# Whole-float32 scores for the first two tiles, and earlier transposes in the first batch of a top-k attention kernel with two feed-forward layers

## The chip, the core and the metric

The kernel runs on one core of a Trainium2 chip. The metric is the device time of one execution in microseconds (us). Engines: PE (TensorE, matrix products and transposes), PEld (its weight loads), DVE (VectorE), ACT (ScalarE), POOL (GpSimd), SP (SyncE, which here only issues transfers).

## What is computed

```python
def _attn_ref(q, k, v):            # (4, 8, 576, 64) each
    scores = scale * np.matmul(q, k.transpose(0, 1, 3, 2))
    kth = np.partition(scores, -32, axis=-1)[..., -32:-31]
    scores = np.where(scores >= kth, scores, -1e9)
    scores = scores - np.max(scores, axis=-1, keepdims=True)
    attn = np.exp(scores)
    attn = attn / (np.sum(attn, axis=-1, keepdims=True) + 1e-09)
    return np.matmul(attn, v)
def _moe_ref(x, w_in, w_out):      # x (2304, 512), w_in (512, 2048), w_out (2048, 512)
    h = np.maximum(x @ w_in, 0.0)
    return h * h @ w_out
def _moe2_ref(x, w_in, w_out):
    h = x @ w_in
    return np.maximum(0.01 * h, h) @ w_out
# reference: _moe2_ref(_moe_ref(rows of _attn_ref)), all float32
```

## The kernel before

Attention. The 8 heads go in 4 pairs of heads. `UNITS` cuts the four batches into runs of rows; a unit with one head pair gives tiles of 128 score rows (576 columns each), 144 in all, and two tiles make one of 72 pairs. A pair has 16 slots. In slots 0 to 13 DVE finds the 32 largest scores of the pair's two tiles, four rounds of MAX8 (`L829`) and three of MATCH_REPLACE8 (`L831`) each. Behind that ACT and POOL drop the other scores and take the exponential (`drop`, `expo_sum`, `L298` to `L303`), PE transposes the result (`pt_main` `L317`, `pt_left` `L330`; ACT copies it out of PSUM), and PE multiplies it with the values.

The scores (`scores`, `L279`) are computed with products of two float32r parts: queries and keys are loaded as float32 (`load_q` `L248`, `load_k` `L204`), and `split_hi` and a subtraction cut each into a high part and the rest, `split_q` and `split_k`. For the first head pair ACT makes the high parts (`L116`) and DVE the rests (`L258`, `L241`). The key tile holds two copies of the 64 rows of a head, one above the other, so that high part and rest lie in the upper and lower 64 partitions, and two products (with `q` high, with `q` rest) give a half tile of scores. ACT copies each half tile out (`L280`). Tiles 0 to 3 are those of the first head pair and the first 256 rows, 0 and 1 of its first head.

Units 0 to 2 (the first batch, `NATIVE` = 3) transpose whole float32 values and multiply them with the values in whole float32 (`av`, `L401`); the result is scaled and becomes the feed-forward's input, `xn` (`L432`) and its parts `xh`, `xl` (`x_out`). The later units scale first (`norm`, `L312`), split what was transposed (`L322`, `L323`) and use split values (`av_split`, `L412`).

Feed-forward. The 2304 rows form six blocks of 512, 256, 384, 512, 256 and 384 rows. A block and layer is 16 steps: products with `w_in` (12 of `L580`), the activation (ACT, POOL or DVE), products with `w_out` one step later (`L618` in layer 0, `L620` in layer 1). The weights arrive as 64-bit floats and are converted on the way in by ACT (`L513`, `L514`, `L523`), DVE (SCALAR_TENSOR_TENSOR, `L518`, `L519`) and POOL (`L526`); block 0 does so, then the results are read back from DRAM. Block 0 is ready with the eighth `xn` (unit 1, last head pair).

What sets the order. Every piece of attention is put in a slot by hand: `at(slot, function, ...)` (`L739` to `L782`). The loop at `L814` goes through the slots, issues what stands in them, and between them as many feed-forward pieces as a rate asks for. When a block becomes ready, feed-forward work that is still open is issued first (`L841`). The framework's scheduler then orders the instructions of each engine by its own estimate, with attention pieces at a higher priority, so the order on an engine is near the order of the slots but not the same. An engine does its instructions strictly in that order.

Of the kernel before, what the change touches and what calls it, by code (L numbers as in the profile page):

```python
# [38 lines left out]


NATIVE = 3

EARLY = (2, 3)
FILL = (2, 245)
# [27 lines left out]
def topk_attention_moe_moe2_kernel(  # L72
# [11 lines left out]
    D = v.shape[-1]  # L84
    P = 128
# [8 lines left out]
    PE, ACT, DVE, POOL, SP = nc.tensor, nc.scalar, nc.vector, nc.gpsimd, nc.sync  # L94
# [31 lines left out]
    uhs = []  # L126
    tiles = []
    for u in units:
        for hp in range(NHP):
            n = u["n"]  # L130
            uh = dict(u=u, hp=hp, n=n, b=u["b"], first=(u["t0"] == 0), ti=len(tiles), idx=len(uhs),
                      c0=P * (hp % 2) if n == 64 else 0)
# [14 lines left out]
    def direct(uh):  # L147
        return uh["b"] not in EARLY
# [4 lines left out]
    def split(uh):  # L153
        return uh["u"]["i"] >= NATIVE

# [35 lines left out]
    def at(slot, fn, *a):  # L191
        events.setdefault(slot, []).append((fn, a))
# [4 lines left out]
    def load_k(b, hp, st):  # L197
        if b in EARLY:
            KT[b, hp] = ahead.tile([P, 2, S], R, tag="KTa", name="KTa", bufs=KPB)
        else:  # L200
            KT[b, hp] = pool.tile([P, 2, S], R, tag="KT", name="KT", bufs=4)
        x = ahead if b in EARLY else pool
        st["k"] = x.tile([P, 2, S], F, tag="kraw", name="kraw", bufs=1 if b in EARLY else KRB)
        SP.dma_start(st["k"], k[b, hp])  # L204

    VT = {}
# [54 lines left out]
    def scores(t, half):  # L261
        uh = t["uh"]
        d = uh["qs"]
        kt = KT[uh["b"], uh["hp"]]
        if half == 0:
            if direct(uh):
                t["s"] = sbufs[t["i"] % NS]
            else:
                t["s"] = ahead.tile([P, S], F, tag="stage", name="stage", bufs=NST)
        ks = slice(half * HALF, (half + 1) * HALF)  # L270
        mm = [(x[:, h, c:c + P], kt[:, h, ks]) for h, c in t["parts"] for x in d]
        if not direct(uh):
            ps = stage_psum.tile([P, 512], F, tag="sp", name="sp", bufs=SPB)
        elif uh["b"] == 0:
            ps = stage_psum.tile([P, 512], F, tag="sd", name="sd", bufs=SDB)
        else:
            ps = bank()
        for i, (l, r) in enumerate(mm):
            PE.matmul(ps[:, 0:HALF], lhsT=l, rhs=r, start=i == 0, stop=i == len(mm) - 1)  # L279
        ACT.activation(t["s"][:, ks], ps[:, 0:HALF], AF.Copy)  # L280
        if half == 1 and not direct(uh):
            t["sd"] = dram.tile([P, S], F, tag=f"sd{t['i']}", name=f"sd{t['i']}")
            SP.dma_start(t["sd"], t["s"])
# [370 lines left out]
    for uh in uhs:  # L654
        b, hp, i = uh["b"], uh["hp"], uh.get("di")
        z = score_slot(uh["ti"])
        if uh["first"] and direct(uh):
            st = {"i": i}
# [8 lines left out]
        if (b, hp) not in vdone or split(uh) and VTB < NHP:  # L667
            assert not uh["u"]["i"] < NATIVE <= units[max(x["i"] for x in units if x["b"] == b)]["i"]
            vdone.add((b, hp))
# [36 lines left out]
    for n, key in enumerate(keys):  # L706
        ks = [(0, load_k, (*key, held[key]))]
# [9 lines left out]
        if n + 1 < len(keys):  # L717
            nk = keys[n + 1]
            ks = [(0, load_k, (*nk, held[nk]))]
# [15 lines left out]
    for p in range(NPAIRS):  # L735
        pr = dict(t=tiles[2 * p:2 * p + 2], p=p)
        pairs.append(pr)
        z = 16 * p
        for i, t in enumerate(pr["t"]):  # L739
            if direct(t["uh"]):  # L740
                at(z - DLEAD + 5 * i, scores, t, 0)
                at(z - DLEAD + 2 + 5 * i, scores, t, 1)
            else:
                at(z - LEAD + i, load_s, t)
            if i == 0:
                at(z + 14, shifts, pr)
            at(z + 14 + i, drop, pr, i)
            at(z + 16 + i, expo_sum, pr, i)
            if split(t["uh"]):
                at(z + 20 + i, norm, pr, i)  # L750
            at(max(z + 20 + 3 * i, z + 21 + i), pt_main, t)
        at(z + 18, recip, pr)
        at(z + 26, pt_left, pr)
    rslot = [None] * len(blocks)

    def rmark(uh, z):
# [6 lines left out]
    for uh in uhs:  # L763
        if split(uh):
            za, z = 16 * (uh["lastA"] // 2) + 30, 16 * (uh["last"] // 2) + 30
            at(za, av_split, uh, 0)
            at(z + 2, av_split, uh, 1)
            z += 4
            at(z, x_out, uh, (0, 1))
            rmark(uh, z)  # L770
            continue
        apart = uh["n"] > P and uh["n"] % P and uh["ti"] % 2 == 0
        for hs in ((0,), (1,)) if apart else ((0, 1),):
            z = 16 * (uh["lastA"] // 2 if hs == (0,) else uh["last"] // 2) + 30
            nq = 2 * len(hs)
            for i in range(nq):
                at(z + i, av, uh, hs, i)
            at(z + nq, x_out, uh, hs)
        z += nq
        if uh["u"]["i"] == NATIVE - 1 and uh["hp"] == NHP - 1:  # L780
            at(z, open_late)
        rmark(uh, z)  # L782
# [30 lines left out]
    last = max(events)  # L813
    while slot <= last:  # L814
        p, i = divmod(slot, 16)
        if slot >= 0 and p < NPAIRS:
            pr = pairs[p]
# [7 lines left out]
            t = pr["t"][x]  # L825
# [79 lines left out]
```

## Time and profile before

| | us |
|---|---|
| runs, median (lowest to highest) | 1217.16 (1215.74 to 1218.06) |
| profiled execution | 1214.43 |
| its span, first to last instruction | 1212.6 |
| PE busy | 1135.6 (94%) |
| DVE busy | 946.5 (78%) |
| ACT busy | 908.9 (75%) |
| POOL busy | 728.1 (60%) |
| mean granted clock of PE | 0.983 of full speed |

The table says that PE is the fullest engine over the whole span. It is a mean over stages: attention alone at first, then attention and feed-forward together, then feed-forward alone. Which engine sets the time is read stage by stage, from the busy time in stretches and from what an engine waited for.

### The profile page before, as it was taken

The page shows a single profiled execution, that of the slowest core. Times are in us where ns is not written, and L with a number is a line of the kernel's source. Part 1 is how long each engine was busy: PE and PEld are TensorE (multiplying, and loading weights), DVE is VectorE, ACT ScalarE, POOL GpSimd, SP SyncE. Part 2 cuts the span into 40 slices and gives each one's busy share as a digit, 9 for nine tenths or more (in the row PEclk, how much of TensorE's full clock was granted, in tenths as well). Part 3 has the DMA queues.
Part 4 walks back from the last instruction along what each step waited for, and adds up shares of the span by engine and source line. Part 5 has one row for each costly group of instructions (what it writes and reads, how often), then busy time and mean ns, then how long its engine had stood idle before and what let it go on. Part 6 is the DMA issues. An engine that isn't in the chain of part 4 may idle for free.

```text
span 1212.6 us, 20357 instructions
## 1 busy us (share of the span) xinstructions
PE 1135.6 (94%) x6388; PEld 992.6 (82%) x6388; DVE 946.5 (78%) x1944; ACT 908.9 (75%) x2019; POOL 728.1 (60%) x868
## 2 busy tenths in 40 slices
PE   4788878999789989999999998999999999999998
PEld 3666765887578879989999996888788899998997
DVE  7999999778888899999999999999999920110122
ACT  6889899989999988887877777777777764334322
POOL 7998977667689985477656684545576642004300
PEclk9999997999989999999999999999999999999999
DMA  9665566878889988889988787667576589879974
GB/s 305 232 224 196 197 197 255 279 273 303 307 281 301 315 281 270 291 283 397 343 297 293 279 274 258 213 221 236 182 233 230 192 270 368 259 247 343 350 253 137
DMA packets 110522, 323.24 MB, mean 267 GB/s; under 512 B 17488, under 2 KB 25680, under 8 KB 110416
## 3 DMA queue, kind: packets, MB, share of 16 engines
q1 hardware_dynamic: 107776, 317.24, 77.1%
q10 hardware_dynamic: 2640, 4.72, 1.1%
q8 instruction: 51, 0.84, 0.3%
q14 instruction: 55, 0.45, 0.1%
HBM read 254.54 MB, written 67.37 MB: 265 GB/s over the span
## 4 chain that ended last, share of the span: by engine, by line
PE 54%; ACT 17%; DVE 12%; DMA 4%; POOL 3%; issue 3%; ACTq 0%; SPq 0%; POOLq 0%; DVEq 0%
PE h L580 22%; PE acc L618 11%; PE acc L620 11%; DVE m L829 5%; DVE w L831 4%; PE att L412 3%; PE att L317 3%; ACT e L303 2%; ACT att L514 2%; ACT e L298 1%; ACT wc L513 1%; PE att L401 1%; ACT s L280 1%; ACT stage L280 1%; DVE PTs L323 1%
## 5 line engine op out<-in xcount | busy, mean ns | idle before, releaser
L580 PE MATMUL h<-xh,wi 128*128 128x512 f32 (+2 forms) x1280 | 349.8, 345 | 10.5 <-ACT gb L598 4.4
L829 DVE MAX8 m<-w 128x8 f32<-128x576 f32 x432 | 313.2, 747 | 1.6
L580 PEld LDWEIGHTS h<-xh,wi 128*128 128x128 f32 x1280 | 227.5, 191 | 39.3 <-ACT gb L598 6.2
L601 POOL TENSOR_TENSOR gl<-ga,gh 128x512 fp32r<-128x512 f32 (+2 forms) x160 | 163.0, 1018 | 118.8 <-ACT gh L600 54.0
L299 POOL TENSOR_TENSOR e<-s,e 128x576 f32<-128x576 f32 x144 | 203.2, 1432 | 26.7 <-ACT e L298 24.2
L831 DVE MATCH_REPLACE8 w<-m,w 128x576 f32<-128x576 f32 x288 | 213.1, 742 | 0.8
L580 PE MATMUL h<-xl,wi 128*128 128x512 f32 (+2 forms) x640 | 206.8, 341 | 2.8 <-DVE xl L632 2.6
L618 PE MATMUL acc<-gh,wo 128*128 128x512 f32 (+2 forms) x768 | 154.8, 341 | 0.4 <-ACT gh L600 0.4
L620 PE MATMUL acc<-wo,gh 128*128 128x512 f32 x576 | 151.1, 397 | 0.7 <-ACT gh L600 0.6
L599 POOL TENSOR_TENSOR ga<-ga,gb 128x512 f32<-128x512 f32 (+2 forms) x80 | 81.3, 1017 | 117.0 <-ACT gb L598 116.6
L618 PEld LDWEIGHTS acc<-gh,wo 128*128 128x128 f32 x768 | 125.0, 189 | 10.6 <-ACT gh L600 1.1
L580 PEld LDWEIGHTS h<-xl,wi 128*128 128x128 f32 x640 | 121.0, 190 | 15.3 <-DVE xl L632 5.1
L600 ACT ACTIVATE gh<-ga 128x512 fp32r<-128x512 f32 (+2 forms) x192 | 100.3, 522 | 35.6 <-POOL ga L599 24.2
L303 ACT ACTIVATE e<-e,kf 128x576 f32<-128x576 f32 x144 | 112.4, 781 | 15.6 <-POOL e L299 14.2
L620 PEld LDWEIGHTS acc<-wo,gh 128*128 128x128 f32 x576 | 104.2, 189 | 19.6 <-ACT gh L600 1.2
L298 ACT ACTIVATE e<-s,kf 128x576 f32<-128x576 f32 x144 | 105.8, 777 | 15.4 <-POOL kf L291 13.5
L829 DVE MAX8 m<-s 128x8 f32<-128x576 f32 x144 | 104.5, 747 | 11.9 <-ACT s L280 10.8
L590 ACT ACTIVATE ga<-h 128x512 f32<-128x512 f32 (+2 forms) x96 | 46.8, 487 | 82.5 <-PE h L580 81.8
L831 DVE MATCH_REPLACE8 w<-m,s 128x576 f32<-128x576 f32 x144 | 106.8, 742 | 0.3
L317 PE MATMUL att<-ident,e 128*128 128x128 f32 x576 | 90.3, 285 | 13.1 <-ACT e L303 9.2
L317 PEld LDWEIGHTS att<-ident,e 128*128 128x128 f32 x576 | 70.6, 145 | 27.4 <-ACT e L303 14.9
L312 ACT ACTIVATE e<-e,rc 128x576 f32<-128x576 f32 x108 | 78.0, 770 | 13.6 <-DVE rc L308 13.5
(93 smaller groups left out, 2150.8 us busy)
## 6 DMA issues: line engine op xcount, KB each, us to landing
wi<-wd SPq DMA_DIRECT2D x160, 512.0 KB, 5.0
wo<-wd SPq DMA_DIRECT2D x160, 512.0 KB, 5.2
wraw<-in_w_dram SPq DMA_DIRECT2D x64, 512.0 KB, 5.7
sd<-stage SPq DMA_DIRECT2D x72, 288.0 KB, 2.8
s<-sd SPq DMA_DIRECT2D x72, 288.0 KB, 5.0
wd<-wi SPq DMA_DIRECT2D x32, 512.0 KB, 5.3
wd<-wo SPq DMA_DIRECT2D x32, 512.0 KB, 5.5
kraw<-in_k_dram SPq DMA_DIRECT2D x16, 576.0 KB, 4.6
```

The lines of the kernel that those rows point to most:

```text
L298: ACT.activation(e, x, AF.Relu, bias=pr["kf"][:, i:i + 1], scale=-FAR)
L299: cur["pool"] = POOL.tensor_tensor(e, x, e, op=OP.subtract)
L303: ACT.activation(e, e, AF.Exp, bias=pr["nb"][:, i:i + 1], scale=0.125, accum_out=pr["sum"][:, i:i + 1])
L317: PE.transpose(ps[:, j * P:(j + 1) * P], t["e"][:, j * P:(j + 1) * P], ident)
L580: PE.matmul(h[:, 0:n], lhsT=wi[:, w, c * P:(c + 1) * P], rhs=x[c][y][:, 0:n], start=cnt == 0, stop=cnt == 3 * NK - 1)
L599: POOL.tensor_tensor(a[:, 0:n], a[:, 0:n], b[:, 0:n], op=OP.subtract)
L600: ACT.activation(gh[:, 0:n], a[:, 0:n], AF.Copy)
L601: (DVE if j >= GLD else POOL).tensor_tensor(gl[:, 0:n], a[:, 0:n], gh.bitcast(F)[:, 0:n], op=OP.subtract)
L618: PE.matmul(acc[c][:, 0:n], lhsT=wo[:, w, cs], rhs=g[:, 0:n], start=first, stop=last)
L620: PE.matmul(acc[c], lhsT=g[:, cs], rhs=wo[:, w, :], start=first, stop=last)
L829: cur["dve"] = DVE.max(out=m8[:, x, 8 * r:8 * r + 8], in_=t["s"] if r == 0 else t["w"])
L831: cur["dve"] = DVE.match_replace(out=t["w"], in_to_replace=m8[:, x, 8 * r:8 * r + 8], in_values=t["s"] if r == 0 else t["w"], imm_value=NEG)
```

## The change

Two edits. First, `load_k` loads the keys of the first head pair in two transfers, one for each head, and keeps the loaded tile; `scores` computes tiles 0 and 1 as one product for each half tile, from the loaded queries and keys in whole float32 (64 partitions), in place of two products of split parts. The split parts are still made, for tiles 2 and 3 and for the later units. Second, in the units of the first batch `pt_main` moves from slots 21 and 23 of a pair to 19 and 21, `pt_left` from 26 to 23, and `av` and `x_out` start four slots earlier (26 instead of 30). In later units `pt_main` of the pair's first tile moves from slot 21 to 20.

```diff
@@ load_k
+        if (b, hp) == (0, 0):
+            uhs[0]["kraw"] = st["k"]
+            for h in range(2):
+                SP.dma_start(st["k"][:, h], k[b, hp, :, h])
+            return
         SP.dma_start(st["k"], k[b, hp])
@@ scores
         mm = [(x[:, h, c:c + P], kt[:, h, ks]) for h, c in t["parts"] for x in d]
+        if t["i"] < WHOLE:                 # WHOLE = 2
+            c = t["i"] * P
+            mm = [(uh["q"][0:D, 0, c:c + P], uh["kraw"][0:D, 0, ks])]
@@ slots of a pair
-            at(max(z + 20 + 3 * i, z + 21 + i), pt_main, t)
+            at(z + (20 if split(t["uh"]) else 19) + (3 if split(t["uh"]) else 2) * i, pt_main, t)
         at(z + 18, recip, pr)
-        at(z + 26, pt_left, pr)
+        at(z + (26 if split(pr["t"][0]["uh"]) else 23), pt_left, pr)
@@ units of the first batch
-            z = 16 * (uh["lastA"] // 2 if hs == (0,) else uh["last"] // 2) + 30
+            z = 16 * (uh["lastA"] // 2 if hs == (0,) else uh["last"] // 2) + 26
```

New lines shift the numbers: `L280` of before is `L291` after, `L829` is `L840`, `L580` is `L591`.

ACT at the very start, before. `q_80` are the first head pair's queries, `q_86` the second's, `KT` the first head pair's split keys, `s_104` and `s_105` the scores of tiles 0 and 1.

```order
L116 ACT_TABLE_LOAD
L116 ACTIVATE q_80<-qraw 128x256 x2
L116 ACTIVATE KT<-kraw 128x576 x2
L116 ACTIVATE q_86<-qraw 128x256 x2
L280 ACTIVATE s_104<-sd 128x288 x2
L280 ACTIVATE s_105<-sd 128x288 x2
```

The same place after:

```order
L118 ACT_TABLE_LOAD
L118 ACTIVATE q_80<-qraw 128x256 x2
L118 ACTIVATE KT<-kraw 128x576
L118 ACTIVATE q_86<-qraw 128x256 x2
L291 ACTIVATE s_104<-sd 128x288
L118 ACTIVATE KT<-kraw 128x576
L291 ACTIVATE s_104<-sd 128x288
L291 ACTIVATE s_105<-sd 128x288 x2
```

The second half of the keys moved behind two query copies and a copy of scores.

DVE before the eighth `xn`, which makes block 0 ready, before. `m` and `w` belong to the top-k, `wc` to the conversion of weights.

```order
L829 MAX m_2842<-w 128x8
L829 MAX m_2556<-w 128x8
L831 MATCH_REPLACE w<-m_2842,w 128x576
L308 RECIPROCAL rc<-sum 128x2
L831 MATCH_REPLACE w<-m_2842,s_105 128x576
L829 MAX m_2842<-w 128x8 x2
L831 MATCH_REPLACE w<-m_2842,w 128x576
L432 TENSOR_TENSOR xn<-att,rb 128x256
L831 MATCH_REPLACE w<-m_2842,w 128x576
L518 SCALAR_TENSOR_TENSOR wc<-att,wc 128x512
```

The same place after:

```order
L842 MATCH_REPLACE w<-m_2892,s_105 128x576
L529 SCALAR_TENSOR_TENSOR wc<-att,wc 128x512 x2
L842 MATCH_REPLACE w<-m_2892,w 128x576
L840 MAX m_2892<-w 128x8
L530 SCALAR_TENSOR_TENSOR wc<-att,wc 128x512 x2
L840 MAX m_2892<-w 128x8
L842 MATCH_REPLACE w<-m_2892,w 128x576
L443 TENSOR_TENSOR xn<-att,rb 128x256
L319 RECIPROCAL rc<-sum 128x2
L842 MATCH_REPLACE w<-m_2892,w 128x576
```

From the program's start to this `xn` there are 261 top-k instructions (MAX and MATCH_REPLACE) in both orders, 8 conversions of weights before and 12 after.

PE around the first transposes of pair 29, before. `e_112` and `e_113` are the pair's two tiles, `h` and `acc` are feed-forward work.

```order
L580 MATMUL h<-xh_2890,wi 128x256 x4
L317 MATMUL att<-ident,e_112 128x128 x4
L618 MATMUL acc<-gh,wo 128x256 x8
L618 MATMUL acc<-gl,wo 128x256 x4
L317 MATMUL att<-ident,e_113 128x128 x4
L279 MATMUL att<-KT,q_80 128x288
```

The same place after:

```order
L423 MATMUL att<-PTs,VT 128x320
L591 MATMUL h<-xh_2867,wi 128x256
L328 MATMUL att<-ident,e_112 128x128 x4
L591 MATMUL h<-xh_2867,wi 128x256
L629 MATMUL acc<-gh,wo 128x256 x7
L290 MATMUL att<-KT,q_80 128x288
```

Counted from the start, 960 feed-forward products (`L580`, `L618`, `L620`) stand before these transposes before and 935 after. At other pairs, counted in the same way (before, after): pair 20: 348, 360; 21: 408, 420; 22: 480, 488; 27: 792, 780; 28: 867, 852; 30: 1020, 1013; 31: 1100, 1088; 36: 1374, 1338; 47: 1962, 1941; 48: 2016, 1995; 49: 2067, 2046; 52: 2163, 2163.

## Rows read from the trace of the kernel before

**Rows 1.** The page, part 1: busy us, share of the span, instructions.

```profile
PE 1135.6 (94%) x6388; PEld 992.6 (82%) x6388; DVE 946.5 (78%) x1944; ACT 908.9 (75%) x2019; POOL 728.1 (60%) x868
```

**Rows 2.** Busy time by stretch: us, each engine, granted clock, DMA share, GB/s.

```profile
210.00:240.00 30.00, 30.00 (x156) 25.21 (x156) 22.19 (x42) 28.55 (x61) 21.77 (x23) 1.00 0.84 281
...
400.00:500.00 100.00, 95.76 (x642) 87.14 (x641) 92.25 (x187) 89.75 (x207) 70.00 (x83) 1.00 0.85 284
...
500.00:600.00 100.00, 98.34 (x667) 92.22 (x666) 98.78 (x210) 80.73 (x189) 66.84 (x88) 1.00 0.93 342
...
1000.00:1100.00 100.00, 100.00 (x653) 99.65 (x652) 12.40 (x24) 40.78 (x91) 9.88 (x14) 1.00 0.85 290
```

**Rows 3.** Timeline, 0 to 10 us: start, us, engine, line, operation, [idle before].

```profile
1.46 0.58 SPq L204 DMA_DIRECT2D kraw<-in_k_dram  x1
...
4.35 0.72 ACT L116 ACTIVATE q<-qraw 128x256 fp32r<-128x256 f32 x2 [2.33 <-DMA qraw<-in_q_dram]
...
6.25 1.25 ACT L116 ACTIVATE KT<-kraw 128x576 fp32r<-128x576 f32 x2 [1.19 <-DMA kraw<-in_k_dram]
...
6.97 1.43 DVE L241 TENSOR_TENSOR KT<-kraw,KT 64x576 fp32r<-64x576 f32 x2 [1.42 <-ACT KT L116]
...
7.42 0.70 ACT L116 ACTIVATE q<-qraw 128x256 fp32r<-128x256 f32 x2
...
7.79 1.24 POOL L118 TENSOR_SCALAR q<-qraw 128x256 fp32r<-128x256 f32 x2 [3.90 <-DMA qraw<-in_q_dram]
...
9.65 0.76 DVE L829 MAX8 m<-s 128x8 f32<-128x576 f32 x1 [1.25 <-ACT s L280]
```

**Rows 4.** Timeline, 202 to 209 us, DVE and PE.

```profile
203.20 0.42 DVE L432 TENSOR_TENSOR xn<-att,rb 128x256 f32<-128x256 f32 x1
...
204.90 1.41 PE L580 MATMUL h<-xh,wi 128*128 128x512 f32 x5 [0.57 <-ACT xh L433]
...
208.17 0.66 PE L317 MATMUL att<-ident,e 128*128 128x128 f32 x4 [0.95 <-DVE wc L519]
```

**Rows 5.** Groups of DVE, 214 to 500 us: xcount | busy us, mean ns | idle.

```profile
L518 DVE SCALAR_TENSOR_TENSOR wc<-att,wc 128x512 uint32<-128x512 uint32 x57 | 38.8, 683 | 25.5 <-ACT att L514 23.8 <-POOL wi L526 1.4
```

**Rows 6.** Line L317, transposes: summary, then their count up to three times.

```profile
L317 PE MATMUL att<-ident,e x576: 269/273/478, 28.1 to 984.8; 128*128 128x128 f32 x192
...
0.00:214.00 214.00, 26.22 (x136) 16.80 (x136) 0.94 0.69 229
...
0.00:440.00 440.00, 37.05 (x208) 26.00 (x208) 0.97 0.78 261
...
0.00:697.00 697.00, 61.02 (x384) 46.55 (x384) 0.98 0.81 278
```

**Rows 7.** Chain that ended last, 690 to 705 us: start, us, what.

```profile
691.07 2.08 PE h L580 x12
...
693.27 2.10 PE acc L620 x9
...
695.84 0.46 ACT PTs L322
...
698.99 2.84 POOL e L299 x2
```

**Rows 8.** Busy time by stretch, at the block change.

```profile
740.00:750.00 10.00, 7.14 (x42) 5.64 (x40) 10.00 (x22) 7.99 (x16) 5.21 (x6) 1.00 0.76 228
...
750.00:760.00 10.00, 7.29 (x29) 5.87 (x30) 9.78 (x22) 5.53 (x11) 1.43 (x3) 0.83 0.66 225
```

**Rows 9.** Busy time by stretch, before the feed-forward starts.

```profile
190.00:195.00 5.00, 3.99 (x13) 2.89 (x13) 5.00 (x11) 5.00 (x10) 3.77 (x3) 0.50 1.02 411
...
195.00:200.00 5.00, 4.94 (x14) 3.21 (x13) 5.00 (x11) 4.06 (x10) 4.96 (x5) 0.61 0.57 224
```

**Rows 10.** Timeline of PE, 189 to 202 us.

```profile
189.95 1.65 PE L580 MATMUL h<-xh,wi 128*128 128x512 f32 x3 [0.95 <-ACT stage L280]
...
195.27 6.30 PE L401 MATMUL att<-PT,VN 128*128 128x256 f32 x18
```

More of the change, by code (lines that the diff above doesn't have):

```diff
@@ L41 @@
 NATIVE = 3
+WHOLE = 2
 EARLY = (2, 3)
```

## The prediction

> **What bounds the kernel now.** I read the summary of engines first, then busy time by stretch, then the chain that ended last, then the timeline at the two places that the change touches. The reader is to see three stages. TensorE (PE) is busy 1135.6 of 1212.6 us [rows 1], so any time saved must come out of its 77 us of idleness or follow an earlier start. Up to about 205 us there is attention alone, and VectorE (DVE), which runs the top-k, sets the pace. From 210 us on the feed-forward work lies between the attention, PE is full (30.00 of 30) and DVE falls to 22.19 of 30; from 500 us both are full (98.34 and 98.78 of 100); at the end only feed-forward work is left and PE is at 100.00 of 100 [rows 2]. The end is a fixed amount of PE work behind the last attention, so a gain must make the attention or the PE queue earlier before that. Which of the two holds between 440 and 700 us is the open question: the chain runs over PE until 695 us and then over POOL [rows 7], though DVE has no slack either.
>
> **The sum's base.** The profiled execution took 1214.43 us (span 1212.6 and 1.8 around it); the median of the three runs, 1217.16, is 2.7 above. I take the terms from the profile and subtract them from the median.
>
> **Part 1, the first two tiles as whole float32.** Removed: eight products of split operands and, for the first tile, their wait for the split keys. Added: four products of whole operands and one more DMA. It is tempting to count the start of PE, 7.8 us, but DVE's queue decides: the first MAX8 (9.65) still stands behind the subtraction of both halves of the keys, which ends at 6.97 + 1.43 = 8.40, so at most the 1.25 us that DVE then waits can go [rows 3]. What is late next is the second half of the keys. Bytes that had landed: 256 KB of queries by 4.35, 832 KB by 6.25 (keys of 576 KB), 1344 KB by 7.79 (two more queries) [rows 3]. In the new order the first half (544 KB) comes by about 5.3, the second head pair's queries (800 KB) by 6.1, the second half (1088 KB) by 7.0: estimates along these three rows. ScalarE (ACT), by the order, then does one key half (to 5.9), two query copies of 0.36 (to 6.85), a score copy of 0.4 (to 7.25), the other half of 0.63 (to 7.9), and DVE's subtraction of 0.72 ends at about 8.65 [rows 3]. So the first MAX8 is at 8.7 instead of 9.65: **-0.9**. Ends: -1.25 if nothing is in the way, -0.4 if the second half lands only at 7.79.
>
> The four new products are not shown by the trace. Nearest are the whole-float32 products with the values: 18 instructions in 6.30 us at a granted clock near 0.6, two for each product, so 0.70 us for 256 columns and 0.79 for 288 [rows 9, 10]. Two of them from 5.3 end at 6.9 and are copied by 8.3, before DVE wants them; at half that price they would be just as hidden. If they cost twice as much they end at 8.5, the copy at 8.9, and a quarter of a microsecond of the gain is lost. The added DMA issue is some 0.6 us on SP's queue [rows 3], and what stands behind it (keys and queries of later head pairs, one load now also waiting for PE to have read the whole queries) comes one or two issues later, up to 1.2 us; the third pair's top-k, over ten microseconds on, hides it. If it didn't, DVE would wait that long once.
>
> **Part 2, transposes and products of the first batch moved by 2 to 4 slots.** In the order the feed-forward's start does not move against the top-k: 261 top-k instructions stand before the eighth `xn`, which completes the first block's input, before and after. So the slots alone are worth nothing there; that `xn` starts at 203.20 with no idle time of DVE before it, so DVE's queue sets it, and the first full step follows at 204.90 [rows 4]. But 12 instead of 8 SCALAR_TENSOR_TENSOR of the weight conversion now stand before it: 4 x 0.683 = 2.7 us [rows 5] in a stretch in which DVE never idles. A part comes back, because PE waits 0.95 us for just such a conversion at 208.17 [rows 4]. **+1.7**; ends 0 (the conversions fall into gaps of DVE) and +2.7.
>
> Then the order of attention against feed-forward on PE. At the first transposes of a pair the changed order has, against before, 12 more feed-forward products done at pairs 20 and 21, but fewer from pair 27 on: 12 to 25 fewer at pairs 27 to 29, 36 at pair 36, and exactly 21 fewer at pairs 47, 48 and 49. Twenty-one is one whole step of the 384-row block, 12 products of 2.08 us and 9 of 2.10 [rows 7]: 4.2 us of PE time that the attention no longer waits for. Pairs 0 to 47 have been transposed by 697 us [rows 6], where the chain leaves PE for POOL [rows 7]. The step isn't saved, it is done later, but there is a place for it: between 740 and 760 us PE idles 5.6 us because the next block isn't ready [rows 8]. So where PE sets the pace up to 697 us, this is **-4.2**. The other end is taken where DVE sets it: DVE is already full from about 440 us, 26 pairs transposed [rows 6]; there the lag is about 14 products (the mean over pairs 27 to 31), of a 256-row block. By the 384-column products (2.08 for 12 [rows 7]) I estimate two thirds of 0.17, 0.12 us each: -1.7. I take -4.2, because the chain, the only view that orders the two, is on PE there.
>
> Sum: -0.9 + 1.7 - 4.2 = **-3.4**, 1217.16 - 3.4 = **1213.8 us**.
>
> **Rivals.**
> *DVE holds from 440 us.* For it: 98.78 busy of 100 from 500 us [rows 2]. Against: the chain. Then -0.9 + 1.7 - 1.7 = -0.9: 1216.3.
>
> *The feed-forward starts earlier after all.* Seventeen pairs are transposed between 28.1 and 214 us [rows 6], 10.9 us for a pair of 16 slots, so four slots are 2.7 us. For it: the products stand earlier, the weights are ready. Against: 261 in both. It would replace the +1.7 by -2.7: -0.9 - 2.7 - 4.2 = -7.8, 1209.4.
>
> *Attention is put behind at pairs 20 to 22 and doesn't recover.* This ends on the slower side. There the order has 12 feed-forward products of 512 columns more before the transposes; nine such took 2.10 us [rows 7], 0.23 each, so PE reaches the attention 12 x 0.23 = 2.8 us later in a stretch where DVE is already down to three quarters [rows 2]. If DVE is what matters from there, its lost time isn't given back: -0.9 + 1.7 + 2.8 = +3.6, 1220.8. It decides if DVE's busy share between 214 and 300 us falls by over 2.4 us and the lag at pair 47 is then used up waiting. Against: PE is the full engine there.
>
> *A low clock at the start of the feed-forward.* From 190 to 195 us the granted clock was 0.50, the 1.2 GHz level, after PE had stood idle before several of its groups, and three feed-forward products took 1.65 us, 0.55 each [rows 9, 10]. If the new order leaves such a gap before the first full step, 12 products cost 12 x (0.55 - 0.23) = 3.8 us more; where DVE holds later on, that is -0.9 + 1.7 + 3.8 - 1.7 = +2.9, 1220.1. The Trainium skill ("TensorE: Matmul & The Clock Gate", section "What's actually happening") says that the throttled clock is the default and activity releases it, so a change that thins out PE's work before a full stretch would pay this; the trace agrees in that the low rows follow idle ones. Against: in the order nothing is taken from PE just before that step.
>
> *The first tile gains nothing,* since the second half of the keys lands later than I estimate: part 1 is 0 and DVE holds: 1217.2.
>
> **How the numbers follow.** This kernel's measurement can't tell less than about 0.2%, 2.4 us, from no change. Forecast 0.40 (0.35 of it beyond 2.4 us, 0.05 within); DVE holds 0.25 (within); earlier start 0.10 (faster); attention behind 0.15 and low clock 0.05 (slower); nothing at the start 0.05 (within). Faster 0.45, same 0.35, slower 0.20. The forecast's own range, with part 1 at either end, the conversions at 0 to 2.7 and the lag at 4.2, is 1211.7 to 1215.3. The range for 8 in 10 goes from 1208.5 (most of the earlier start) to 1220.5 (some of the slower cases): DVE idles 7.8 us in each of the stretches 210 to 240 and 400 to 500 [rows 2], and the many small moves of the order there can give or take a few of them.
>
> **What would show it.** The first MAX8 at 8.4 to 9.2 us, with the second key half's copy as what it follows; at 9.6 part 1 is wrong. The eighth `xn` at about 205.0 (203.2 - 0.9 + 2.7), later than before though its products stand earlier; at 201 the second rival is right. Pair 47 transposed by about 693.5 instead of 697, and PE's idleness at the block change near 740 to 760 us down from 5.6 to about 1.4 us: that is the step that decides. If it stays at 5.6 and the last stretch is shifted by only a microsecond, DVE holds. Rows with a doubled price in the first ten products after 205 us would show the clock.

## The result, and the profile after

The changed kernel takes 1227.37 us (median of 6 runs, 1225.32 to 1229.59), the kernel before beside it 1217.61 (6 runs): a ratio of 1.0073, interval 1.0055 to 1.0092. It is 9.8 us slower, where 3.4 us faster was forecast; the range ended at 1220.5. The profiled execution took 1229.59 us, its span is 1227.8, 15.2 more than before. The profile before is one of that kernel's shorter executions and the profile after the longest of its six, so differences between the two traces carry some 5 us more than the medians do.

In this execution the start came out as forecast. The timeline of the changed kernel, 0 to 10 us (start, us, engine, line, operation, idle before):

```profile
1.44 0.58 SPq L209 DMA_DIRECT2D kraw<-in_k_dram  x1
...
2.67 0.60 SPq L209 DMA_DIRECT2D kraw<-in_k_dram  x1
...
4.69 2.25 PE L290 MATMUL sd<-kraw,qraw 64*128 64x288 f32 x4 [4.69 <-DMA kraw<-in_k_dram]
...
7.00 0.67 ACT L118 ACTIVATE KT<-kraw 128x576 fp32r<-128x576 f32 x1
...
7.70 0.90 DVE L248 TENSOR_TENSOR KT<-kraw,KT 64x576 fp32r<-64x576 f32 x1 [1.66 <-ACT KT L118]
...
8.64 0.76 DVE L840 MAX8 m<-s 128x8 f32<-128x576 f32 x1
```

The first MAX8 stands at 8.64 instead of 9.65 [rows 3], behind the second half of the keys. That difference is not shown to be the edit's. The same row of the kernel before, unchanged, in its second execution, and of the first edit alone:

```profile
9.07 0.76 DVE L829 MAX8 m<-s 128x8 f32<-128x576 f32 x1 [1.25 <-ACT s L280]
...
9.22 0.76 DVE L840 MAX8 m<-s 128x8 f32<-128x576 f32 x1
```

Over the ten traces with the first edit this row stands at 9.27 in the mean (8.64 to 9.97), over the ten without it at 9.26 (8.96 to 9.68).

Then the eighth `xn` and the first full feed-forward step, in the timeline at 209 to 212 us:

```profile
209.54 0.41 DVE L443 TENSOR_TENSOR xn<-att,rb 128x256 f32<-128x256 f32 x1
...
211.30 2.03 PE L591 MATMUL h<-xh,wi 128*128 128x512 f32 x5 [0.63 <-ACT xh L444]
```

Both are 6.4 us later than before (203.20 and 204.90 [rows 4]). Where they went is read from what DVE waited for between 30 and 212 us. (`rc` holds the reciprocals of the sums, `rb` their transposed copy, by which `xn` is scaled; `kf` is the bound below which scores are dropped.) Before (engine, tile, line, what it waited for: us in total, times, longest):

```profile
DVE xn L432 <- ACT rb L366: 1.3, 1, 1.3
DVE rc L308 <- POOL sum L307: 0.6, 1, 0.6
DVE m L829 <- POOL kf L291: 0.5, 1, 0.5
```

After:

```profile
DVE xn L443 <- ACT rb L377: 4.6, 2, 2.8
DVE rc L319 <- POOL sum L318: 1.4, 3, 0.8
DVE m L840 <- POOL kf L302: 1.3, 4, 0.6
```

All rows of the view sum to 3.0 us before and to 7.3 after. So the eighth `xn` is accounted for: 203.2 - 0.4 (DVE has done 0.4 us more by 30 us, which is all that is left by then of the earlier MAX8) + 2.7 (four more conversions ahead of it) + 4.3 (more waiting) = 209.8, measured 209.5. Busy time by stretch says the same. Before (us, PE, PEld, DVE, ACT, POOL, granted clock, DMA share, GB/s):

```profile
0.00:30.00 30.00, 13.83 (x54) 11.36 (x54) 22.50 (x47) 18.13 (x42) 23.82 (x54) 0.97 0.97 304
30.00:212.00 182.00, 152.98 (x827) 120.76 (x827) 178.37 (x381) 164.52 (x436) 155.93 (x198) 0.94 0.65 217
212.00:300.00 88.00, 86.90 (x442) 71.99 (x441) 66.75 (x125) 81.47 (x173) 61.35 (x61) 1.00 0.84 285
300.00:500.00 200.00, 185.99 (x1055) 159.03 (x1054) 177.16 (x345) 184.27 (x398) 151.76 (x159) 0.98 0.86 291
500.00:700.00 200.00, 197.23 (x1249) 186.31 (x1249) 197.92 (x420) 158.25 (x351) 131.69 (x167) 0.99 0.88 312
```

After:

```profile
0.00:30.00 30.00, 16.28 (x52) 12.25 (x53) 22.89 (x47) 17.15 (x39) 23.67 (x54) 0.96 0.89 262
30.00:212.00 182.00, 154.63 (x801) 124.85 (x801) 174.06 (x374) 163.10 (x432) 154.39 (x197) 0.87 0.65 220
212.00:300.00 88.00, 86.63 (x432) 71.67 (x431) 61.31 (x116) 77.43 (x164) 56.92 (x58) 0.98 0.78 278
300.00:500.00 200.00, 183.96 (x989) 153.78 (x988) 173.96 (x336) 182.26 (x388) 152.27 (x157) 0.97 0.83 280
500.00:700.00 200.00, 194.92 (x1256) 182.87 (x1255) 197.50 (x418) 157.42 (x354) 126.35 (x164) 0.99 0.85 303
...
185.00:205.00 20.00, 15.38 (x49) 11.43 (x48) 19.63 (x42) 19.60 (x46) 15.41 (x16) 0.50 0.78 279
...
210.00:240.00 30.00, 29.24 (x144) 23.89 (x145) 22.85 (x45) 26.32 (x57) 19.09 (x21) 0.94 0.72 247
```

Between 30 and 212 us DVE does 4.3 us less, between 212 and 300 us 5.4 less, between 300 and 500 us 3.2 less. With the 0.4 more at the start it is 9.4 us behind by 300 us and 13.0 by 700 us, where the spans of these two traces end 15.2 apart. Its work in all is unchanged (946.5 us before, 945.6 after), so that work comes later, and after 500 us, where DVE and PE have both no slack [rows 2], nothing is given back. Between 212 and 300 us the waits are again of many kinds, for instance in the timeline after:

```profile
256.56 0.17 DVE L319 RECIPROCAL rc<-sum 128x2 f32<-128x2 f32 x1 [3.33 <-POOL sum L318]
258.58 0.23 DVE L443 TENSOR_TENSOR xn<-att,rb 128x64 f32<-128x64 f32 x1 [1.85 <-PE att L412]
...
299.27 0.69 DVE L334 TENSOR_TENSOR PTs<-att,PTs 128x512 fp32r<-128x512 f32 x1 [3.73 <-ACT PTs L333]
```

The largest single wait before 212 us shows how one comes about. After, 142 to 157 us:

```profile
142.19 1.13 ACT L291 ACTIVATE stage<-sp 128x288 f32<-128x288 f32 x3 [1.90 <-DMA sd<-stage]
...
142.66 1.38 PE L290 MATMUL sp<-KTa,q 128*128 128x288 f32 x6 [1.80 <-ACT stage L291]
...
147.92 2.52 PE L412 MATMUL att<-PT,VN 128*128 128x256 f32 x10
...
151.80 2.52 PE L412 MATMUL att<-PT,VN 128*128 128x256 f32 x10
...
154.62 0.38 PE L362 MATMUL att<-ident,rc 128*128 128x128 f32 x2
...
155.30 0.38 ACT L377 ACTIVATE rb<-att 64x256 f32<-64x256 f32 x1
...
155.71 0.42 DVE L443 TENSOR_TENSOR xn<-att,rb 128x256 f32<-128x256 f32 x1 [2.85 <-ACT rb L377]
...
156.05 1.41 DVE L840 MAX8 m<-w 128x8 f32<-128x576 f32 x2
```

Before, the same place:

```profile
148.45 2.52 PE L401 MATMUL att<-PT,VN 128*128 128x256 f32 x10
...
151.27 0.38 PE L351 MATMUL att<-ident,rc 128*128 128x128 f32 x2
...
152.37 0.38 ACT L366 ACTIVATE rb<-att 64x256 f32<-64x256 f32 x1
...
152.78 0.42 DVE L432 TENSOR_TENSOR xn<-att,rb 128x256 f32<-128x256 f32 x1
```

This `xn`, the sixth, stands in DVE's queue behind 198 top-k instructions before and 196 after, nearly the same place, but the second ten products and the transposes of `rc` behind them come 3.4 us later on PE, although their slots are earlier. Part of that is read in the first two rows: ahead of them on PE stand scores of later batches, which wait 1.80 us for ACT, and ACT waits 1.90 us for the staging tile to be written to DRAM; in the trace before there is no such wait for a transfer between 126 and 148 us. DVE reaches `xn`, finds `rb` missing, and the top-k behind it stands still for 2.85 us. The Trainium skill ("PSUM — Partial Sum Buffer", section "Engine vs sequencer instructions") says that the queues of ScalarE, VectorE and GpSimd are strictly first in, first out; this row agrees, for the MAX8 behind `xn` had its input and starts only at 156.05.

The late step, after. Transposes up to 697 us (line `L328`: PE, PEld, clock); then the last eight of pair 47 in PE's timeline, before and after; then the block change, now some 14 us later:

```profile
0.00:697.00 697.00, 63.07 (x375) 47.92 (x376) 0.95 0.79 270
```

```profile
695.20 1.04 PE L317 MATMUL att<-ident,e 128*128 128x128 f32 x8
...
708.93 1.04 PE L328 MATMUL att<-ident,e 128*128 128x128 f32 x8
```

```profile
760.00:770.00 10.00, 7.49 (x37) 5.64 (x36) 9.83 (x21) 8.25 (x18) 4.92 (x6) 0.91 0.79 220
770.00:780.00 10.00, 9.31 (x37) 7.22 (x36) 9.93 (x23) 7.78 (x15) 4.49 (x5) 0.92 0.81 276
```

375 transposes instead of 384 [rows 6], pair 47 done 13.7 us later, and 3.2 us of idle PE at the block change instead of 5.6 [rows 8].

### The profile page after: what moved, and what is told of

The parts are those of the page before. It is cut to its first block, busy times and chain, and to the rows that moved or that the text cites. A ratio compares the mean times of both kernels' runs of the same rounds, so it can differ in the third digit from the quotient of the medians.

```text
span 1227.8 us, 20345 instructions
## 1 busy us (share of the span) xinstructions
PE 1152.6 (94%) x6388; PEld 1005.8 (82%) x6388; DVE 945.6 (77%) x1944; ACT 909.8 (74%) x2019; POOL 727.3 (59%) x868
## 4 chain that ended last, share of the span: by engine, by line
PE 49%; DVE 9%; POOL 1%; ACT 1%; issue 1%; DMA 0%; ACTq 0%; POOLq 0%
PE h L591 22%; PE acc L631 11%; PE acc L629 10%; DVE m L840 4%; PE att L423 3%; DVE w L842 3%; PE att L328 2%; DVE PTs L334 1%; PE att L341 1%; DVE xl L643 0%; PE att L290 0%; DVE PTs L351 0%; POOL gl L612 0%; POOL e L310 0%; DMA out_dram<-y 0%
## 5 line engine op out<-in xcount | busy, mean ns | idle before, releaser
L591 PE MATMUL h<-xh,wi 128*128 128x512 f32 (+2 forms) x1280 | 352.9, 348 | 11.1 <-ACT ga L601 3.0
L840 DVE MAX8 m<-w 128x8 f32<-128x576 f32 x432 | 313.0, 747 | 1.4
L591 PEld LDWEIGHTS h<-xh,wi 128*128 128x128 f32 x1280 | 229.0, 192 | 38.8 <-ACT ga L601 4.1
L591 PE MATMUL h<-xl,wi 128*128 128x512 f32 (+2 forms) x640 | 209.0, 344 | 3.6 <-DVE xl L643 3.4
L591 PEld LDWEIGHTS h<-xl,wi 128*128 128x128 f32 x640 | 122.2, 192 | 17.5 <-DVE xl L643 5.9
L840 DVE MAX8 m<-s 128x8 f32<-128x576 f32 x144 | 104.8, 747 | 6.8 <-ACT s L291 4.5
L328 PE MATMUL att<-ident,e 128*128 128x128 f32 x576 | 94.3, 289 | 11.5 <-ACT e L314 6.5
L328 PEld LDWEIGHTS att<-ident,e 128*128 128x128 f32 x576 | 73.4, 148 | 23.7 <-ACT e L314 10.7
L290 PE MATMUL sp<-KTa,q 128*128 128x288 f32 x320 | 72.6, 355 | 20.0 <-ACT stage L291 14.8
```

Source lines behind the costliest of these rows:

```text
L328: PE.transpose(ps[:, j * P:(j + 1) * P], t["e"][:, j * P:(j + 1) * P], ident)
L591: PE.matmul(h[:, 0:n], lhsT=wi[:, w, c * P:(c + 1) * P], rhs=x[c][y][:, 0:n], start=cnt == 0, stop=cnt == 3 * NK - 1)
L840: cur["dve"] = DVE.max(out=m8[:, x, 8 * r:8 * r + 8], in_=t["s"] if r == 0 else t["w"])
```

## The experiments

The letters in an expectation stand for the theories that it names itself; from the third group of runs on, A is "what the edits move forward costs the time" and B "the order of the queues as a whole does, not a piece". Times are medians in us, each beside the kernel before on the same chip (1215.96 to 1218.68 in the five groups). "DVE early" and "DVE late" are DVE's busy us between 30 and 212 and between 212 and 300 us in the profile of that run.

| kernel | median (runs) | ratio and interval | span | DVE early | DVE late |
|---|---|---|---|---|---|
| before | 1217.61 (6) | | 1212.6 | 178.37 | 66.75 |
| changed | 1227.37 (6) | 1.0073 (1.0055 to 1.0092) | 1227.8 | 174.06 | 61.31 |
| first edit alone | 1220.76 (10) | 1.0029 (1.0019 to 1.0040) | 1219.2 | 174.72 | 63.27 |
| second edit alone | 1224.34 (5) | 1.0048 (1.0031 to 1.0064) | 1222.2 | 177.76 | 62.73 |
| only later units' slot | 1221.00 (7) | 1.0026 (1.0010 to 1.0043) | 1218.9 | 178.28 | 64.34 |
| only products and `x_out` | 1220.20 (10) | 1.0018 (1.0004 to 1.0032) | 1217.7 | 177.49 | 63.19 |
| changed, later units back | 1229.52 (4) | 1.0091 (1.0069 to 1.0114) | 1226.7 | 173.90 | 64.30 |
| changed, `x_out` back | 1226.86 (4) | 1.0077 (1.0048 to 1.0106) | 1225.3 | 171.77 | 65.59 |
| changed, conversions back | 1233.80 (4) | 1.0137 (1.0114 to 1.0160) | 1233.7 | 171.58 | 62.92 |
| before, product doubled | 1216.83 (10) | 0.9998 (0.9978 to 1.0017) | 1214.6 | 176.00 | 65.00 |
| changed, product doubled | 1228.07 (4) | 1.0094 (1.0060 to 1.0129) | 1231.0 | 174.68 | 60.82 |
| before, 29 slots | 1222.82 (4) | 1.0072 (1.0048 to 1.0096) | 1219.0 | 178.07 | 63.14 |
| changed, 29 slots | 1226.90 (4) | 1.0096 (1.0081 to 1.0111) | 1225.3 | 173.05 | 61.80 |
| before, 31 slots | 1227.32 (6) | 1.0081 (1.0055 to 1.0107) | 1226.0 | 171.87 | 60.57 |
| changed, 31 slots | 1222.36 (10) | 1.0029 (1.0012 to 1.0046) | 1221.0 | 175.60 | 62.30 |
| before, 32 slots | 1219.27 (6) | 1.0027 (1.0013 to 1.0042) | 1216.6 | 175.65 | 66.75 |
| changed, 32 slots | 1216.69 (10) | 1.0003 (0.9986 to 1.0021) | 1215.8 | 175.87 | 67.18 |
| before, 33 slots | 1215.57 (10) | 0.9988 (0.9972 to 1.0003) | 1211.8 | 176.39 | 68.33 |
| changed, 33 slots | 1222.53 (8) | 1.0043 (1.0029 to 1.0056) | 1217.3 | 176.50 | 67.53 |

**Each edit alone.** First edit (the slots as before):

```
-            at(z + (20 if split(t["uh"]) else 19) + (3 if split(t["uh"]) else 2) * i, pt_main, t)
+            at(max(z + 20 + 3 * i, z + 21 + i), pt_main, t)      # pt_left 26, av 30 too
```

> The kernel before with the first edit alone: tiles 0 and 1 in whole float32 and the first keys in two transfers; all slots as before. Theory (the moved slots make the change slow): the first MAX8 at 8.6 to 8.7 us as in the changed kernel, the eighth xn within 2 us of 203.2, and a time of 1214 to 1218. Rival A (the first edit itself costs, by what it does to loads and clock in the first 60 us): 1221 to 1228. Rival B (any reordering moves the time by several us either way, whatever the edit): no time is excluded, and the eighth xn does not tell it.

Measured +3.0 us, over the theory's range and just under rival A's. The early MAX8 is not there (9.22, where 8.6 to 8.7 was expected), and the eighth `xn` is at 205.16, 2 us late. Second edit alone (`WHOLE` and the two key loads left out):

```
-        if t["i"] < WHOLE:
-            c = t["i"] * P
-            mm = [(uh["q"][0:D, 0, c:c + P], uh["kraw"][0:D, 0, ks])]
```

> The kernel before with all moved slots and without the first edit. Theory (the slots make it slow): the eighth xn at 206 to 211 us, the feed-forward 3 to 8 us late from there on, a time of 1222 to 1229. Rival A (the first edit costs): 1215 to 1219.

Measured +6.6 us, inside the theory's range, but without its sign: the eighth `xn` is at 202.65, not at 206 to 211, with four top-k instructions fewer ahead of it than before. Here the loss is behind 212 us (DVE early 177.76, DVE late 62.73). The two edits alone add up to what both cost, 9.6 and 9.8, but by the next runs that is an accident.

**Pieces of the second edit.** Before, with only the later units' slot (21 to 20):

```
-            at(max(z + 20 + 3 * i, z + 21 + i), pt_main, t)
+            at(z + (20 + 3 * i if split(t["uh"]) else 21 + 2 * i), pt_main, t)
```

> The kernel before, with only the first transposes of the later units' pairs one slot earlier (20 instead of 21). The order up to the eighth xn is that of before. Theory (the loss is in the first batch): 1214 to 1220. Rival (these transposes hold PE): 1221 to 1226, with PE waiting before L317 for ACT's scaled tile.

Measured +3.3. This order has the same 21 fewer feed-forward products at pair 47, and no gain. The rival's sign is missing too: before `L317` PE waits 1.9 us for the scaled tiles, 1.3 in the kernel before. The same piece taken out of the changed kernel:

```
-            at(z + (20 if split(t["uh"]) else 19) + (3 if split(t["uh"]) else 2) * i, pt_main, t)
+            at(z + (21 if split(t["uh"]) else 19) + 2 * i, pt_main, t)
```

> The changed kernel, but the first transposes of the later units' pairs stand in slot 21 again, as before the change; the first batch as in the change. Theory (the loss arises before the feed-forward starts, in the first batch): the eighth xn late as in the changed kernel (209 to 210) and a time within 4 us of the changed kernel's 1227. Rival (the transposes one slot earlier in the 54 later pairs wait for the scaled tile and hold PE): the loss after 214 us goes, 1218 to 1222.

Measured 1229.5, no gain back: what costs 3 us in one order costs nothing in another. Before, with only the products and `x_out` four slots earlier (30 to 26). The loads and conversions of the first weights are placed from that slot (`rslot`), so they move forward with it, here and in the change itself:

> The kernel before with one piece of the second edit alone: the products with values and `x_out` of the first batch start at slot 26 in place of 30; transposes and scores as before. Theory A (the loss comes with what the edits move forward: products, `x_out` and with them the weight conversions, which now stand ahead of the top-k): all slots cost 6.5 us against 1217.6 and the later units' shift alone 3.3, so this piece should show the remaining 3 us, 1220.5 to 1221.5. Theory B (no single piece costs it: each new order of the queues falls into or out of stalls of its own, as the unrelated order with its +10 us did): anything from 1216 to 1228, with no relation to the 3 us.

Measured +1.5, under what A asked.

**Is it what stands ahead of the top-k?** Changed kernel, `x_out` at its old slot:

```
-            at(z + nq, x_out, uh, hs)
-        z += nq
+            at(z + nq + 4, x_out, uh, hs)
+        z += nq + 4
```

> The changed kernel with `x_out` of the first batch back at its old slot (products stay four slots forward). `x_out` sets the slot at which the first block counts as ready, so the weight conversions and the feed-forward's rate go back with it. Theory A: of 1227.4 the share of conversions and early `xn` comes back, some 3 to 6 us: 1221.5 to 1224.5, with the eighth `xn` 3 us earlier than the 209.5 of the changed kernel. Theory B: another order, another draw: 1217 to 1229; whatever it is, the time goes with the eighth `xn` and with the idle time of DVE between 212 and 300 us, not with the slot.

Measured 1226.9: A is wrong here. The order leaves the sixth `xn` where it was (behind 196 top-k instructions), and it waits again:

```profile
156.06 0.43 DVE L443 TENSOR_TENSOR xn<-att,rb 128x256 f32<-128x256 f32 x1 [2.81 <-ACT rb L377]
```

The eighth `xn` is at 208.97, 0.6 us earlier instead of 3.

Changed kernel, loads, conversions and stores of the first weights four slots later, where they stood before:

```
-    at(rslot[0] - 28, convert_now, 0)
+    at(rslot[0] - 24, convert_now, 0)      # the other five lines too
```

> The changed kernel with only the loads, conversions and stores of the first weights back at their old slots (four later than in the changed kernel); `x_out` and the products stay forward. The order still has 12 conversions before the eighth `xn`, but three top-k instructions fewer. Theory A: conversions are ahead of the top-k in the changed kernel and cost 2.7 us there, so 1 to 3 us come back: 1224.5 to 1226.5. Theory B: 1217 to 1229, not bound to the conversions.

Measured 1233.8, 6 us slower than the changed kernel: A said faster, and it lies above B's range as well. No piece that is put back gives time back.

**Controls.** The kernel before, unchanged, once more:

> The kernel before, unchanged, for a second profile: how far the moments of the eighth xn and of the later blocks move between two executions of one order. All theories: the eighth xn within 1 us of 203.2; if it moves by more, the differences shown between traces have to be read with that width.

One run, 1216.74 us, span 1214.0. The eighth `xn` is at 203.57 (0.4 us later), DVE early 177.51 and DVE late 66.89, 0.7 us less in sum than in the first execution. So these two executions of one order agree within a microsecond up to 300 us. That is two of them: beside this run the kernel before took 1213.06 to 1223.31 over 15 runs, and a single trace can differ by more. Then the first product of every half tile that goes through the staging banks issued twice, in the changed kernel and in the kernel before:

```
+        if not direct(uh):
+            PE.matmul(ps[:, 0:HALF], lhsT=mm[0][0], rhs=mm[0][1], start=True, stop=True)
```

> The changed kernel, with the first product of every staged score half tile issued twice (the first result is overwritten): 144 more short products on PE before and during the feed-forward's start, meant to keep PE's clock up. Theory C (the lower granted clock of PE in the first 210 us, 0.81 to 0.94 where before had 0.92 to 1.0, is what makes DVE wait): the clock there rises by 0.05 or more, the eighth xn comes 2 to 5 us earlier than 209.5, time 1219 to 1225. Theory O (the order, not the clock): eighth xn 207 to 212, time 1225 to 1231.

> The control: the kernel before with the same doubled products. Theory C: no slower, 1213 to 1218. Theory O: another order, 1219 to 1224.

144 more instructions on PE, all before 212 us, change nothing in either (1228.1 and 1216.8). In the changed kernel the granted clock between 30 and 212 us rises from 0.87 to 0.92, as theory C asked, but the eighth `xn` stands at 210.88 and no time comes back, so C is not borne out; the second run misses what O expected of it. The single wait of 2.85 us is also gone in the first of these runs (the sixth `xn` waits 0.93 us), yet DVE early is nearly the same (174.68) and so is the time. So PE's own work before 205 us is covered, and thinner PE work ahead of the feed-forward isn't what the change lost.

**A change without content.** `DLEAD`, the number of slots by which scores and their loads are issued ahead of the top-k, 30 in both kernels, is set to 29, 31, 32 and 33, with and without the two edits. It holds for the tiles of the first two batches; the expectations say every tile, but those of the last two batches are computed early, at other slots:

```
-DLEAD = 30
+DLEAD = 31
```

> The kernel before with scores issued one slot earlier everywhere (lead 31 instead of 30): neither of the change's edits, but another order on every engine. Theory S (what is lost is what these edits do at their places): 1214.5 to 1219.5. Theory O (another order than the one before costs by itself some 3 us, as two runs so far showed +3 for quite different edits): 1219.5 to 1224, with more waiting of DVE between 210 and 300 us than the 19.9 us of before.

> A null change of the changed kernel: all edits stay, only the scores of every tile are issued one slot earlier (31 slots ahead in place of 30), which cost the kernel before 9.9 us. Theory A (the edits themselves cost 9.8 us, wherever the rest stands): 1226 to 1230 or, if both add, 1237. Theory B (the kernel before sits in an order that is better than its neighbours, and both edits and the shifted scores lose the same thing once): at or below the changed kernel, anything from 1217 to 1229, and not 1237.

> The kernel before with the scores of every tile issued 29 slots ahead in place of 30. Theory A (the edits cost about 10 us by themselves, and the null change that cost 9.9 us was an accident): 1216 to 1220. Theory B (the kernel before sits in one good order; most of its neighbours are some us slower for waits of DVE ahead of and just behind the first block's start): 1219 to 1228. With it goes the time: the later its eighth `xn` and the more DVE waits between 30 and 300 us over the 22.7 us of before, the slower.

> The changed kernel with the scores 29 slots ahead; pairs with the kernel before at 29. Theory A: about 10 us above its pair, 1226 to 1230. Theory B: no fixed distance to its pair; over 29, 30, 31 and 32 slots the mean of the four differences (so far +9.8 at 30, -5.0 at 31) is within some 4 us of zero. It has the same early order as the changed kernel, so the `xn` that waited 2.85 us near 156 us should wait again and the eighth `xn` stand near 208 to 210: 1224 to 1230.

> The kernel before with the scores 32 slots ahead. Theory A: 1216 to 1220, or like 31 slots (1227) if earlier scores cost by themselves. Theory B: 1219 to 1228, neither fixed by 30 nor by 31 slots.

> The changed kernel with the scores 32 slots ahead; pairs with the kernel before at 32. Theory A: about 10 us above its pair. Theory B: no fixed distance; its early order is that of the changed kernel at 31 slots, which had no long wait at 156 us and came out at 1222.4, so 1219 to 1225.

> The kernel before with the scores 33 slots ahead; a fifth pair. The pairs so far (with the edits minus without): +4.1 at 29, +9.8 at 30, -6.2 at 31, -2.6 at 32, a mean of +1.3; without the edits the settings stand at 0 to +9.9 over 1217. If the order decides: 1217 to 1228.

> The changed kernel with the scores 33 slots ahead. The edits by themselves: a fixed 10 us above its pair. The order: no fixed distance, 1216 to 1228, and the mean of five pairs within 4 us of zero. At 32 it was level with the kernel before; a version below 1214 would beat both kernels.

The edits cost, changed minus before at the same setting and each against its own runs of the kernel before: +4.1 at 29, +9.8 at 30, -6.2 at 31, -2.6 at 32, +7.0 at 33. The mean is +2.4, its standard error 3.0 (from the scatter of the five, 6.7). One slot of `DLEAD`, which adds and removes nothing, moves the kernel before by up to 9.9 us (30 to 31), and the five settings lie 12.2 us apart without rising or falling steadily (+6.9, 0, +9.9, +3.3, -2.3). So theory A, a fixed cost of some 10 us, is wrong: the same edits cost 7.0 us in one order and save 6.2 in another. A small cost of their own is neither shown nor excluded. Expectations missed here: the kernel before at 31 slots (1227.3) lies above both of its ranges; 31 slots with the edits might have reached 1237 by A and came to 1222.4; the changed kernel at 32 slots came 2.3 us under its span of 1219, the kernel before at 33 slots 1.4 us under its 1217. Five runs lie in B's ranges, two of them (the kernel before at 32 slots, the changed one at 29) in A's as well.

The time goes with what DVE has done by 300 us, not with the eighth `xn` alone (202.26 at 29 slots without the edits, 6.9 us slower; 203.85 at 33, 2.3 us faster). Busy time by stretch, changed kernel at 31 slots, where the long wait at 156 us is gone:

```profile
30.00:212.00 182.00, 155.25 (x806) 124.12 (x805) 175.60 (x379) 163.53 (x433) 155.04 (x197) 0.90 0.66 220
212.00:300.00 88.00, 87.09 (x437) 72.24 (x435) 62.30 (x115) 78.81 (x165) 57.78 (x57) 0.99 0.80 277
```

Its timeline has the transposes of `rc` at 152.11, and both `xn` follow:

```profile
152.11 0.43 PE L362 MATMUL att<-ident,rc 128*128 128x128 f32 x2
...
153.72 0.41 DVE L443 TENSOR_TENSOR xn<-att,rb 128x256 f32<-128x256 f32 x1
...
205.62 0.41 DVE L443 TENSOR_TENSOR xn<-att,rb 128x256 f32<-128x256 f32 x1
```

The changed kernel at 32 slots, level with the kernel before, and the kernel before at 31 slots, 9.9 us slower:

```profile
30.00:212.00 182.00, 154.70 (x802) 123.25 (x802) 175.87 (x377) 162.40 (x431) 155.30 (x196) 0.88 0.66 221
212.00:300.00 88.00, 86.21 (x440) 71.69 (x439) 67.18 (x124) 80.94 (x170) 57.79 (x57) 0.98 0.80 280
```

```profile
30.00:212.00 182.00, 152.13 (x800) 120.70 (x799) 171.87 (x368) 159.95 (x426) 152.11 (x194) 0.90 0.61 208
212.00:300.00 88.00, 85.02 (x403) 70.27 (x402) 60.57 (x117) 74.83 (x156) 54.79 (x55) 0.92 0.75 249
```

The slow one, without any edit, has the same kind of wait as the changed kernel, at another unit:

```profile
76.19 0.42 DVE L432 TENSOR_TENSOR xn<-att,rb 128x256 f32<-128x256 f32 x1 [3.58 <-ACT rb L366]
```

Over the 19 rows of the table the correlation of span and DVE's busy time from 30 to 300 us is -0.87, with 1.4 us of span for each us that DVE lacks by then; taken to 500 us it is -0.93, with 1.1 us. That is a connection and not an experiment: no run took one wait away and left the rest of the order as it was, since each edit that was tried moved hundreds of instructions. That these waits cost the time is argued from it, not shown.

No version beat the kernel before beyond doubt. The best, the kernel before at 33 slots, has an interval of 0.9972 to 1.0003.

## Why the prediction was wrong

**Part 1, -0.9 at the start: met in this trace by luck.** The first MAX8 came at 8.64 (8.7 forecast), behind the second key half as said. But it comes as early in no other trace, and with the edit it stands no earlier in the mean than without it (9.27 and 9.26). The forecast took the loads from one execution: the second head pair's queries, which ACT copies ahead of the second key half, were put at 6.1; ACT goes on with them at 6.08 here, at 6.64 with the first edit alone and at 6.92 at 31 slots. The kernel before moves likewise, 9.65 and 9.07 in two executions. So no run shows a gain of 0.9 at the end, and the first edit alone is 3.0 us slower. The new products were dearer than taken, 2.25 us for four instructions, so 1.1 us for one product of 288 columns instead of 0.79, but the first MAX8 did not wait for them.

**Part 2, +1.7 at the eighth `xn`: a right term beside a missing one.** Four more conversions and their 2.7 us were there. Missing was the waiting of DVE, +4.3 us between 30 and 212 us. The sum took durations from the trace of before and counts from the order, and assumed that DVE would idle as little as before, "a stretch in which DVE never idles". That was a property of one order.

**The step that failed, -4.2 at pair 47.** "4.2 us of PE time that the attention no longer waits for" holds only if the attention is there to use it. The step took PE as what sets the pace up to 697 us, and put new waits of DVE at nothing. The attention was 13.7 us late by then (708.93 instead of 695.20, forecast 3.5 us earlier), DVE's work being 13.0 us behind, so the fewer products ahead of it bought nothing. The other orders show that the lag by itself is no gain: with only the later units' slot the same 21 products are missing at pair 47 and the kernel is 3.3 us slower; the kernel before has 1941 products there at 31 slots too, 9.9 us slower, and at 33 slots, 2.3 us faster; the changed kernel at 32 slots has 1983, more than before, and is level. What the forecast had right is that this moment decides: from pair 47's transposes to the end all 20 traces take 513.5 to 522.4 us. Idle PE at the block change did shrink, by 2.4 us instead of 4.2, but behind a later start.

**The rivals.** *Attention put behind and not recovering* had the right side and the right sign to look for: DVE's busy time in the stretch from 212 us fell by 5.4, over the 2.4 that was set as its point. Its price was too small, and its place too narrow: it was put on 12 products at pairs 20 to 22, while nearly half of what DVE loses by 300 us is lost before 212 us, in waits for `rb`, `sum` and `kf`, and more follows after 300 us. It had a chance of 0.15. *Low clock*: the granted clock did fall, 0.87 instead of 0.94 between 30 and 212 us, with 0.50, the lower level (1.2 GHz), from 185 to 205 us; but the changed kernel at 32 slots has 0.88 there and is level with the kernel before, and the doubled products raised the clock to 0.92 for no gain, so it doesn't decide. Its sign behind 205 us is there in part: the first five products take 2.03 us instead of 1.41 [rows 4]. At 32 slots with the edits the same five take 2.33. *Feed-forward earlier* is wrong, +6.4 us. *DVE holds* fits in that the time goes with DVE's work, but it counted on no new waits of DVE. *The first tile gains nothing* had part 1 right in the mean of the traces; it missed the rest.

**The range.** It priced the moves that could be named, one by one. The runs at 29 to 33 slots show what was not priced: an order that differs in hundreds of places is some 5 us off by itself (-2.3 to +9.9 without the edits, +0.7 to +10.9 with them).

**What stays open.** Which of the new waits cost the 9.8 us, and what makes the scheduler's order of the kernel before, or of the changed one at 32 slots, low in waits, isn't settled, nor whether the edits in the mean cost anything (+2.4, give or take 8 at 95% with five pairs).

## What to carry to other kernels

When a scheduler turns a small edit into a new order of whole queues, first measure a few orders that differ by nothing that matters, and take their scatter as the least range of a forecast; one pair of before and after can't tell an edit's cost from it. And read a moment that hangs on the first loads from more than one execution before it becomes a term. An instruction moved forward on one engine only helps if its inputs come forward too: in a queue that is done in order it otherwise holds up all that is behind it, so look in the trace for the last input (here a small copy behind twenty products), not for the large one. A gain ahead of such a queue counts only as far as the queue doesn't wait later for something else.

## What was not expected of the hardware

Whole-float32 scores of 64 partitions take two instructions for each product and some 0.56 us for each of them at the start (2.25 us for four). And 144 further products on PE, in a kernel whose PE is 94% busy over the span, cost nothing that can be measured (ratio 0.9998, interval 0.9978 to 1.0017). All of them lie before 212 us; without them PE is busy 152.98 of the 182 us from 30 to 212, DVE 178.37.
